# Two channel-major quarters instead of three in some blocks, and Gram products issued one slot after their block

## The chip, the cores and the metric

The kernel runs on one NeuronCore of one Trainium2 chip. A core has a matrix engine (TensorE, PE in the profile, with its weight loads listed apart as PEld), a vector engine (VectorE, DVE), an activation engine (ScalarE, ACT), a general engine (GpSimd, POOL) and a queue engine that only issues transfers (SyncE, SP). Each engine works through its own instructions in order and waits on semaphores for the others. Matrix products land in PSUM, which has eight banks of 128 x 512 fp32; ACT and DVE read them from there.

The metric is device time in microseconds. Smaller is better.

## What is computed

This is one ConvNeXt-V2 block on an image of 512 x 512 pixels with C = 96 channels and E = 384 hidden channels, all in bf16:

```python
out = depthwise 3x3 convolution of x                 # 9 taps, 96 channels
h = (out - mean) / sqrt(var + 1e-5)                   # over the 96 channels of a pixel
h = gelu(h @ w1)                                      # 96 -> 384
gx = sqrt((h * h).sum(over all pixels) + 1e-6)        # one number per hidden channel
nx = gx / (gx.mean(over channels) + 1e-6)
h = grn_gamma * (h * nx) + grn_beta + h
return x + h @ w2                                     # 384 -> 96
```

The line that shapes everything is `gx`: the sum of squares of every hidden channel over the whole image has to be known before the second product can start. So the kernel has a first pass, which ends in `gx`, and a second pass, which makes the output.

## The kernel before

**Blocks and quarters.** The image is cut into 128 blocks of 4 rows (2048 pixels). A block's hidden activations are four quarters of 512 pixels by 384 channels. A quarter is made in one of two layouts. *Channel-major*: hidden channels on the partitions, pixels along the free axis, three products of 128 x 512 with `w1p` stationary. *Pixel-major*: pixels on the partitions, channels along the free axis, six products (384, 128, 256, 256, 128 and 384 columns) with the normalised pixels stationary.

**Two ways to sum squares.** For a channel-major quarter DVE runs three `bn_stats` over 128 x 512 (`entry`, line 672; tile `bst`), which hold mean and variance of 512 pixels. For a pixel-major quarter PE multiplies the activations by themselves: for each of four groups of 128 pixels and each of three groups of channels it issues one 128 x 128 product with the same tile as stationary and as moving operand, and adds it into `gram` in PSUM bank 7; the diagonal is the sum of squares. `gram_next` (line 768) issues such products. One entry of its list `grams` stands for two groups of pixels, so for six products. A pixel-major quarter leaves two entries, twelve products.

**Which block has which.** `cm_quads` (line 100) gives the number of channel-major quarters of block q. Among blocks below 112 it depends on the last digit of q: digits 0, 3, 7 have four ("whole" blocks, whose activations are also stored to memory); digits 1, 4, 8 have two; digits 2, 5, 6, 9 have three. The list of last digits is called a cycle here: ten blocks, ten slots.

**Slots.** The first pass is a loop over slots (`for s in range(last_slot + 1)`). In the steady part a slot does the convolution of block s and the MLP of block s - 14, and the order of the instructions on PE and ACT is written out by hand in the loop's `else` branch: `conv(0)`, `unit(0, 2)`, `unit(2, 1)`, `conv(1)`, `unit(3, 1)`, `unit(4, 2)`, Gram products, `unit(6, 1)`, `unit(7, 1)`, `conv(2)`, `evac`, Gram products, `unit(8, 2)`, `unit(10, 1)`, the sums for the layer norm (`stage_stats`, 24 small products), `unit(11, 1)`. A `unit(bank, n)` fills n PSUM banks with products of the MLP, and ACT applies gelu to them into tile `g`. Units of two banks always use banks 0 and 1; units of one bank take banks 2 and 3 in turn. Each `conv(n)` is a third of the taps (24 products of 64 x 32) into `Y3`, banks 4 to 6, of which there is one copy only: the next slot's `conv(0)` can start when `evac` has copied the banks that it writes into `y_bf`.

**Who copies.** In most slots ACT copies all of `Y3` (128 x 1536). Where the slot's MLP block has two channel-major quarters (`shared`), ACT copies banks 4 and 5 (128 x 1024) and DVE copies bank 6 (128 x 512, the `CAST` rows).

**DVE's order in a slot.** `squares(0)` (2 bn_stats), two transposes of the input for the convolution three slots ahead (`turn_x`), `squares(1)` (2), the copy of bank 6 where shared, `squares(2)` (2), then `squares_rest(2)` (3, if the block has a third channel-major quarter) and the three that a whole block in the slot before still owes. With three in place of four quarters' worth in the slot of a whole block, every slot of a cycle has nine.

**Gram products in a slot.** Each of the two `gram_next` calls takes one entry off the list (six products). A cycle leaves 3 blocks x 4 + 4 blocks x 2 = 20 entries and takes 20, two in each slot; a block's products come up to two slots after it.

**Accounts.** The results of `bn_stats` are kept in groups of 32 entries; when a group is full, `aggregate` condenses it. With `NENT` = 370 entries there are twelve groups, and a thirteenth for the last two blocks. `second_moments`, near the end of the first pass, works over all groups but the last.

**Second pass.** Whole blocks are read back, five blocks are held, and the rest are computed again from the normalised pixels. Its order doesn't depend on `cm_quads` except through which blocks are whole.

In the profile all engine calls of the first pass have the line of a helper (L35), so groups are told apart by operation, tile and shape.

Of the kernel before, what the change touches and what calls it, by code (L numbers as in the profile page):

```python
# [17 lines left out]
BATCH = 4  # L18
NHELD = 5
WHOLE = (0, 3, 7)  # L20
NTAIL = 14
GRB = 3

# [33 lines left out]
def kernel(  # L57
# [23 lines left out]
    NBLK = H // GR  # L81
# [7 lines left out]

    TAIL0 = NBLK - NTAIL  # L90
    HELD = [NBLK - 2 - 2 * i for i in range(NHELD)][::-1]
    KEPT = [NBLK - 5, NBLK - 3, NBLK - 1]

    def is_held(q):
        return q in HELD

    def is_whole(q):
        return q < TAIL0 and q % 10 in WHOLE

    def cm_quads(q):  # L100
        if is_whole(q) or is_held(q):
            return NQ
        if q > HELD[0]:
            return 1
        return 2 if q >= NBLK - 16 or (q - 1) % 10 in WHOLE else 3

    whole = [q for q in range(NBLK) if is_whole(q)]
    g_dram = dram.tile([len(whole), 128, NQ * NCH * QW], bf16, name="g_dram")
# [78 lines left out]
    with ExitStack() as p1:  # L187
# [426 lines left out]
        def stage_rows(k):  # L614
            b0, n = BATCHES[k]
            rt = rts.pop(k)
            N = n * GR * NG
            nq, nt = min(32, N), (N + 31) // 32
            with nc.allow_non_contiguous_dma("small rows of rstd"):
                if nq == 32:  # L620
                    for t in range(nt):
                        sp.dma_start(
                            out=r_dram[b0:b0 + n].rearrange("b r w -> (b r w)").rearrange(
                                "(t q a p) -> t a q p", q=32, a=4, p=32)[t],
                            in_=rt[:, 32 * t:32 * t + 32])
                else:
                    for a in range(4):
                        sp.dma_start(
                            out=r_dram[b0:b0 + n].rearrange("b r (g m) -> (b r g) m", g=NG)[:, 32 * a:32 * a + 32],
                            in_=rt[32 * a:32 * a + nq, :32])  # L630

        def stage_bcast(k):
            b0, n = BATCHES[k]
            rbc = rbcpool.tile([128, BATCH, W], bf16, name="rbc")
            for j in range(GR):
                sp.dma_start(out=rbc[32 * j:32 * j + 32, :n, :].rearrange("p n w -> p (n w)"),
                             in_=bass.AP(r_dram[b0].tensor, r_dram[b0].offset + j * n * W, [[0, 32], [1, n * W]]))
            rbcs[k] = rbc
# [30 lines left out]
        def flat(b):  # L669
            return gs[b].rearrange("p t j w -> p (t j w)")  # L670
# [91 lines left out]
        def square_owed():  # L762
            while owed:
                owed.pop()()

        grams = []

        def gram_next(n):
            for b, c0 in grams[:n]:
                for c1 in (c0, c0 + E):  # L770
                    for j in range(NCH):
                        v = flat(b)[:, c1 + j * 128:c1 + j * 128 + 128]
                        pe.matmul(gram[:, j, :], lhsT=v, rhs=v, start=False, stop=True, skip_group_check=True)
            del grams[:n]
# [63 lines left out]
        for s in range(last_slot + 1):  # L838
            get = lambda kind: at.get((s, kind), [])
            for k in get("rows"):  # L840
                stage_rows(k)
            for k in get("bcast"):
                stage_bcast(k)
            if s + 4 < NBLK:
                load_x(s + 4)
            for b in get("read"):
                stage_read(b)
            for b in get("write"):
                stage_write(b)
            store_next()  # L850
            for k in get("newton"):
                stage_newton(k, pool)
            for b in get("sqp"):
                stage_sq(b, False)
            for b in get("norm"):
                stage_norm(b)
            for k in get("rstd"):
                stage_rstd(k, pool)
            mlp = get("mlp")

            def spread_out():
                for k in get("spread"):
                    stage_spread(k)
                for b in get("norma"):
                    stage_norm(b, dve if b < 2 else pool)

            spare = not mlp and s % 2 == 1
            taps, evac = conv_taps(s, spare) if s < NBLK else ([], None)
            if mlp and mlp[0] >= TAIL0:
                assert not taps  # L870
                square_owed()
                mlp_tail(mlp[0], get)
            elif not mlp:
                if s + 3 < NBLK:
                    turn_x(s + 3)
                for f in taps:
                    f()
                if not spare:
                    spread_out()
                if evac:  # L880
                    evac()
                for b in get("sqa"):
                    stage_sq(b, True)
                for b in get("stats"):
                    stage_stats(b)
                for k in get("moments"):
                    stage_moments(k)
                if spare:
                    spread_out()
                for k in get("chain"):  # L890
                    stage_moments(k)
                    stage_chain(k)
                for k in get("turn"):
                    stage_turn(k)
                gram_next(2)
                square_owed()
            else:
                b = mlp[0]
                unit, squares, squares_rest = mlp_units(b)
                conv = lambda n, fence=True: taps[n](fence) if taps else None  # L900

                conv(0)
                unit(0, 2)
                unit(2, 1)
                squares(0)
                conv(1, False)
                spread_out()
                if s + 3 < NBLK:
                    turn_x(s + 3)
                unit(3, 1)  # L910
                unit(4, 2)
                squares(1)
                gram_next(1 if taps else 2)
                shared = evac is not None and cm_quads(b) == 2
                unit(6, 1)
                if not shared:
                    squares(2)
                unit(7, 1)
                for k in get("turn"):
                    stage_turn(k)  # L920
                conv(2)
                if evac:
                    evac(shared)
                if shared:
                    squares(2)
                gram_next(1 if taps else 2)
                unit(8, 2)
                unit(10, 1)
                for b2 in get("stats"):
                    stage_stats(b2)  # L930
                unit(11, 1)
                for k in get("moments"):
                    stage_moments(k)
                squares_rest(2)
                square_owed()
                if is_whole(b):
                    owed.append(lambda f=squares_rest: f(3))
                grams.extend((b, c) for c in range(cm_quads(b) * QC, NQ * QC, 2 * E))
                if is_whole(b):
                    stores.extend((b, h) for h in range(3))  # L940
            if s == 0:
                setup_ynt()
            if s == 3:
                setup_mlp()
            if s == 4:
                setup_rest()
            if s == 6:
                for i in range(NI):
                    sp.dma_start(out=w1s[i:128:4], in_=w1p[i:C:NI])
            for b in get("combine"):  # L950
                combine(b)
            if s == last_slot - 3:
                pc.close()
                late.xr = p2.enter_context(tc.tile_pool(name="xr", side="right", bufs=5))
                late.xb = p2.enter_context(tc.tile_pool(name="xb", side="right", bufs=3))
                late.gr = p2.enter_context(tc.tile_pool(name="gr", side="right", bufs=GRB))
                late.gl = p2.enter_context(tc.tile_pool(name="gld", side="right", bufs=2))
                late.o = p2.enter_context(tc.tile_pool(name="o", side="right", bufs=4))
            if s == last_slot - 2:
                for n in range(PRE):  # L960
                    load_xr(n, sp)
                second_moments(0, NACC - 1)
            if s == last_slot - 1:
                for n in range(3):
                    stage_xb(ORDER[n], pool, B2bc_f)
            if s == last_slot:
                for n in range(PRE):
                    load_rest(n, sp, sp)
# [102 lines left out]
```

## Time and profile before

| what | value |
|---|---|
| median of 3 runs | 1471.92 us (1469.99 to 1472.07) |
| the profiled execution's own time | 1470.01 us |
| its span in the profile | 1468.2 us |
| mean granted TensorE clock | 0.995 |
| PE busy over the span | 1392.9 us (95%) |
| ACT busy over the span | 1404.5 us (96%) |
| POOL busy over the span | 1300.0 us (89%) |
| DVE busy over the span | 1187.7 us (81%) |
| DVE `bn_stats`, 128 x 512 | 1110, 673.5 us busy |
| PE Gram products, 128 x 128 (`PS<-g`) | 1464, 123.4 us busy |
| DVE copies of bank 6 (`CAST y_bf<-PS`) | 35, 23.5 us busy |

The shares of busy time are averages over two passes with different limits. The first pass ends with the first products of the second at about 964 us; its steady part, with a convolution and an MLP in every slot, lies between about 200 and 867 us. There a slot starts with the first of three rows `MATMUL PS<-xT,Wq ... x24` in the time-ordered view of PE and ends where the next slot's first such row starts.

### The profile page before, as it was taken

What the parts mean: (1) busy time and instruction counts of PE and PEld (TensorE: products, weight loads), DVE (VectorE), ACT (ScalarE), POOL (GpSimd) and SP (SyncE); (2) the same over time, 40 slices, a digit from 0 to 9 for tenths busy, and PEclk for the clock granted to TensorE, in tenths of its full rate; (3) what the DMA queues carried; (4) which work ended last, traced back from release to release, by engine and by line L of the source; (5) the groups of instructions that cost most, each with busy time, mean ns of one, the idle gap of its engine ahead of it and who ended that gap; (6) DMA issues with size and microseconds to landing.
All of it is one profiled execution on the core that took longest, in us unless ns stands there. A gap on an engine that the chain in (4) does not pass through costs nothing.

```text
span 1468.2 us, 54503 instructions
## 1 busy us (share of the span) xinstructions
PE 1392.9 (95%) x23125; PEld 811.3 (55%) x23125; DVE 1187.7 (81%) x2174; ACT 1404.5 (96%) x1595; POOL 1300.0 (89%) x923
## 2 busy tenths in 40 slices
PE   8889999999999999999999998779999999999998
PEld 3434444444444444444444455557777777777776
DVE  8859989999999999999999997965555555555555
ACT  7889999999999999999999999989999999999997
POOL 3479889999999999999899997449999999999998
PEclk9999999999999999999999999999999999999999
DMA  6578878788888888888889876649999999999998
GB/s 181 178 218 241 264 236 279 244 262 262 266 263 275 259 250 269 266 272 255 269 246 284 256 226 200 197 161 375 358 329 387 396 390 399 400 385 408 385 395 311
DMA packets 167914, 422.03 MB, mean 287 GB/s; under 512 B 34327, under 2 KB 84183, under 8 KB 163191
## 3 DMA queue, kind: packets, MB, share of 16 engines
q1 hardware_dynamic: 151428, 314.98, 66.1%
q0 software_dynamic: 14880, 103.43, 18.6%
q8 instruction: 181, 2.97, 0.8%
q14 instruction: 63, 0.51, 0.1%
q10 hardware_dynamic: 1362, 0.15, 0.1%
HBM read 262.16 MB, written 156.22 MB: 285 GB/s over the span
## 4 chain that ended last, share of the span: by engine, by line
DVE 36%; PE 28%; POOL 14%; ACT 13%; issue 4%; DMA 2%; SPq 2%; ACTq 0%; POOLq 0%; DVEq 0%
PE PS L35 28%; DVE bst L35 25%; POOL xb L328 11%; ACT g L35 9%; DVE xT L35 7%; ACT y_bf L35 3%; SPq L35 2%; POOL xr L283 1%; DVE y_bf L35 1%; DMA yn_dram<-yn 1%; POOL yn L35 1%; DVE o_sb L35 1%; DMA ynT<-yn_dram 1%; ACT xT L35 1%; DVE parts L35 1%
## 5 line engine op out<-in xcount | busy, mean ns | idle before, releaser
L35 ACT ACTIVATE g<-PS 128x512 bf16<-128x512 f32 (+2 forms) x1062 | 730.0, 845 | 12.9 <-PE PS L35 9.9
L35 DVE BATCH_NORM_STATS2 bst<-g 128x6 f32<-128x512 bf16 x1110 | 673.5, 673 | 26.2 <-ACT g L35 26.0
L35 ACT ACTIVATE gr<-PS 128x1536 bf16<-128x1536 f32 x360 | 498.5, 1457 | 20.8 <-PE PS L35 9.7
L35 DVE TENSOR_TENSOR o_sb<-PS,xb 128x384 bf16<-128x384 f32 x512 | 277.6, 556 | 222.0 <-PE PS L35 170.0
L35 POOL TENSOR_TENSOR yn<-y_bf,rbc 128x1536 bf16<-128x1536 bf16 x126 | 391.0, 3106 | 45.4 <-ACT rbc L35 21.7
L328 POOL TENSOR_TENSOR xb<-xr,B2c 128x1536 f32<-128x1536 bf16 x118 | 368.2, 3133 | 1.5
L35 PE MATMUL PS<-xT,Wq 64*32 64x511 bf16 (+1 forms) x9198 | 345.4, 387 | 21.7 <-ACT y_bf L35 6.4
L35 PE MATMUL PS<-ynT,w1p 128*128 128x512 bf16 x1161 | 332.5, 383 | 22.9 <-ACT g L35 5.4
L35 POOL TENSOR_TENSOR ysq<-y_bf 128x1536 bf16<-128x1536 bf16 x114 | 313.0, 2746 | 30.7 <-ACT y_bf L35 16.7
L35 PE MATMUL PS<-ynT,w1s 128*128 128x512 bf16 x1020 | 275.6, 379 | 0.0
L35 PEld LDWEIGHTS <-gr 128*128 128x128 bf16 x4296 | 212.5, 98 | 61.3 <-issue 3.2
L35 PE MATMUL PS<-W2s,gr 128*128 128x96 bf16 x4224 | 223.8, 206 | 1.9 <-DVE o_sb L35 1.8
L35 PEld LDWEIGHTS <-Wq 64*32 64x32 bf16 x9216 | 111.7, 90 | 191.1 <-issue 148.8
L35 ACT ACTIVATE y_bf<-PS 128x1536 bf16<-128x1536 f32 (+2 forms) x135 | 182.1, 1354 | 16.8 <-PE PS L35 12.6
L35 DVE STREAM_TRANSPOSE xT<-xin 128x576 f32<-128x576 f32 (+1 forms) x256 | 181.6, 749 | 14.7 <-DMA xin<-in_x_dram 14.7
L35 PEld LDWEIGHTS <-w1p 128*128 128x128 bf16 x1161 | 89.9, 98 | 178.9 <-issue 116.0
L35 PEld LDWEIGHTS <-g 128*128 128x128 bf16 (+1 forms) x1707 | 105.7, 98 | 88.3 <-issue 56.1
L35 PE MATMUL PS<-w1p,ynT 128*128 128x256 bf16 (+2 forms) x822 | 125.7, 273 | 7.7 <-ACT xT L35 3.2
L35 PE MATMUL PS<-g 128*128 128x128 bf16 x1464 | 123.4, 221 | 3.5 <-DVE PS L35 3.5
L35 PEld LDWEIGHTS <-w1s 128*128 128x128 bf16 x1020 | 82.0, 98 | 40.5
L35 PEld LDWEIGHTS <-gl 128*128 128x128 bf16 x1680 | 83.1, 98 | 29.7 <-issue 8.5
L35 PE MATMUL PS<-W2s,gl 128*128 128x96 bf16 x1680 | 90.3, 206 | 5.0 <-DVE o_sb L35 4.3
(109 smaller groups left out, 714.1 us busy)
## 6 DMA issues: line engine op xcount, KB each, us to landing
xin<-in_x_dram SPq DMA_DIRECT2D x126, 432.0 KB
g_dram<-g SPq DMA_DIRECT2D x105, 512.0 KB
gl<-g_dram POOLq DMA_DIRECT2D x35, 1536.0 KB, 10.9
yn_dram<-yn SPq DMA_DIRECT2D x512, 96.0 KB
ynT<-yn_dram SPq DMA_DIRECT2D x128, 384.0 KB
out_dram<-o_sb SPq DMA_DIRECT2D x127, 384.0 KB
xr<-in_x_dram POOLq DMA_DIRECT2D x123, 384.0 KB, 6.8
ynT<-yn_dram SPq DMA_DIRECT2D x255, 128.0 KB
```

The lines of the kernel that those rows point to most:

```text
L35: r = f(*a, **k)
L283: pq.dma_start(out=xr[:], in_=x[0, r0:r0 + GR].rearrange("r w c -> (r w) c").rearrange("(p g) c -> p g c", g=PXP))
L328: pq.tensor_tensor(out=xb[:], in0=grp[q]["xr"][:], in1=bias[:, None, :].to_broadcast([128, PXP, C]), op=ALU.add)
```

## The change

`cm_quads` gets a list of its own for blocks with two channel-major quarters: last digits 1, 4, 5, 8, 9. So digits 5 and 9 go from three to two, and only 2 and 6 have three. Below block 112 this concerns 22 blocks. In their slots, `shared` is now true too. The two calls of `gram_next` no longer take one entry each: the first takes half of what is on the list (rounded up), the second the rest.

```diff
+TWOS = (1, 4, 5, 8, 9)
...
-        return 2 if q >= NBLK - 16 or (q - 1) % 10 in WHOLE else 3
+        return 2 if q >= NBLK - 16 or q % 10 in TWOS else 3
...
                 squares(1)
-                gram_next(1 if taps else 2)
+                gram_next((len(grams) + 1) // 2)
                 shared = evac is not None and cm_quads(b) == 2
                 unit(6, 1)
...
                 if shared:
                     squares(2)
-                gram_next(1 if taps else 2)
+                gram_next(len(grams))
                 unit(8, 2)
```

A cycle now leaves 5 blocks x 4 + 2 blocks x 2 = 24 entries. Since the list is empty at the end of every slot's second call, a slot issues what the block before it left. By the last digit of the slot's MLP block:

| digit | 0 | 1 | 2 | 3 | 4 | 5 | 6 | 7 | 8 | 9 |
|---|---|---|---|---|---|---|---|---|---|---|
| channel-major quarters before | 4 | 2 | 3 | 4 | 2 | 3 | 3 | 4 | 2 | 3 |
| channel-major quarters after | 4 | 2 | 3 | 4 | 2 | 2 | 3 | 4 | 2 | 2 |
| Gram entries in the slot before | 2 | 2 | 2 | 2 | 2 | 2 | 2 | 2 | 2 | 2 |
| Gram entries in the slot after | 4 | 0 | 4 | 2 | 0 | 4 | 4 | 2 | 0 | 4 |

`NENT` falls from 370 to 348, and with it the groups from twelve and one to eleven and one.

## The prediction

> **What bounds the kernel now.** I first took the busy times of the engines by stretches of 100 us. From 300 to 800 us every stretch looks like this one (columns: PE, PEld, DVE, ACT, POOL busy, granted clock, DMA):
>
> ```profile
> 500.00:600.00 100.00, 97.15 (x1769) 47.52 (x1765) 99.69 (x176) 99.05 (x144) 93.65 (x77) 1.00 0.86 262
> ```
>
> Four engines are nearly full, so the average names no bound. The chain that ended last, for 500 to 560 us, names DVE:
>
> ```profile
> by line: DVE bst L35 68.1%; DVE xT L35 20.2%; issue 4.7%; DVE y_bf L35 2.9%; DVE mom L35 1.4%; PE PS L35 1.3%; DVE rt L35 0.6%; DVE PS L35 0.6%; DVE tot L35 0.5%
> ```
>
> A chain can run along any engine that is full, so I then read PE slot by slot. First the slot of a two-quarter block:
>
> ```profile
> 500.83 0.89 PE L35 MATMUL PS<-xT,Wq 64*32 64x512 bf16 x24
> ...
> 504.08 0.50 PE L35 MATMUL PS<-g 128*128 128x128 bf16 x6
> 504.41 0.60 PE L35 MATMUL PS<-w1p,ynT 128*128 128x384 bf16 x4
> 504.94 0.87 PE L35 MATMUL PS<-xT,Wq 64*32 64x512 bf16 x24
> 505.74 0.51 PE L35 MATMUL PS<-g 128*128 128x128 bf16 x6
> 506.09 0.82 PE L35 MATMUL PS<-w1p,ynT 128*128 128x128 bf16 x6
> ```
>
> The next slot starts at 507.65, so this one lasted 6.82 us, without a stated wait: PE is the limit. Each six Gram products move what follows by 0.33 to 0.35 us. Slots that copy all of `Y3` on ACT last 7.03 us; from 514.92:
>
> ```profile
> 521.42 0.38 PE L35 MATMUL PS<-ynT,w1p 128*128 128x512 bf16 x1
> 521.95 0.88 PE L35 MATMUL PS<-xT,Wq 64*32 64x512 bf16 x24 [0.16 <-ACT y_bf L35]
> ```
>
> Here PE is done early and waits for ACT's copy (520.35, 1.55 us long, so to 521.90). This is a loop, not a full engine: taps, first unit, six gelu calls, copy, next taps.
>
> DVE comes in at one place, its copy of bank 6, which it reaches late:
>
> ```profile
> 509.07 0.65 DVE L35 CAST y_bf<-PS 128x512 bf16<-128x512 f32 x1
> ...
> 509.40 1.27 PE L35 MATMUL PS<-xT,Wq 64*32 64x512 bf16 x24
> ```
>
> The second row of taps needs that bank; it takes 1.27 instead of 0.88 us, and the slot from 507.65 7.27 us. The nine cycles from 213.34 to 846.15 (starts of the slots of blocks 20 and 110) average 70.3 us. With undisturbed slots (7.03 four times; three times each 6.82 and the 6.98 of the slot behind it when DVE is on time, as from 578.23 to 585.21) a cycle would be 69.5: DVE costs 0.8 us per cycle.
>
> Last, a slot that already has what the change makes three times a cycle, a two-quarter block without any Gram product:
>
> ```profile
> 199.70 0.89 PE L35 MATMUL PS<-xT,Wq 64*32 64x512 bf16 x24 [0.67 <-ACT y_bf L35]
> ...
> 203.00 0.87 PE L35 MATMUL PS<-w1p,ynT 128*128 128x384 bf16 x4
> 203.81 0.88 PE L35 MATMUL PS<-xT,Wq 64*32 64x512 bf16 x24
> 204.62 0.83 PE L35 MATMUL PS<-w1p,ynT 128*128 128x128 bf16 x6
> 205.28 0.45 PE L35 MATMUL PS<-rowsel,y_bf 128*128 128x4 bf16 x12
> ```
>
> and the next slot begins at 206.31. It lasted 6.61, not 6.82 - 0.67 = 6.15: ACT's short copy (205.07, 1.18 us long, to 206.25) holds the next taps. PE's lead is lost there.
>
> **The change part by part.**
>
> *DVE.* Each of 22 blocks loses three bn_stats and gains one copy of bank 6. Nine bn_stats in a row take 5.40 us with one of 0.67 at the end, so 0.59 each from start to start, and the copy as much: -1.19 us per block, -26 us in all. The stretch of nine cycles has DVE busy 630.5 of 632.8 us, 70.1 per cycle; it becomes 67.7. DVE is then no longer late, and the 0.8 us per cycle of waits goes; what is late next is PE and the copy loop, so no more than that is gained. In undisturbed slots the copy starts about 0.1 us into the next slot and a start up to 1.0 us there delays nothing, which is the cover for the two further copies; if it is gone, each costs 0.4 us as above.
>
> *ACT.* 22 copies shrink from 128x1536 to 128x1024. ACT's wait for PE grows instead; the gain is that `Y3` is free sooner, which counts only where PE isn't the limit.
>
> *PE, quarters.* Three products of 512 columns become six with as many columns; the two layouts cost the same (0.65 us per quarter, from start to start): nothing. Its six weight loads in place of three lie beside products.
>
> *PE, Gram products.* Twelve more per changed block, 264 in all; and the four entries of a block now fall into one slot. Within a six the starts are (0.50 - 0.22)/5 = 0.056 us apart, and six move the rest by 0.33; twelve more in a slot cost 0.67. No row shows twelve in a run. The lower end is 0.66, two sixes at 0.33, and nothing at all if the 6.82 held a wait that they could fill, for which no row speaks. The upper end is 0.88, from the chain's first piece of the second pass, where 627 products of mixed shapes, most of them with a new stationary tile each, take 45.95 us, 0.073 each. I take 0.67, since shape and stage are the same. The Trainium skill, "TensorE: Matmul & The Clock Gate", section on the back-to-back issue gap, says that in a stream of loads and products the spacing at 128 columns is about 81 ns, with 56 ns only for isolated ones; this trace has 56 in such a stream of six. By 81 ns the heavy slots below would be 0.3 us longer, and the estimate some 17 us higher.
>
> *Slots of the changed cycle.* Heavy slots (digits 0, 2, 5, 6, 9; four entries): PE's own work, 6.80 (6.79 to 6.82 in slots where PE is the limit), + 0.67 = 7.47. Is anything else later? The first six extra products put `unit(6, 1)` at 504.41 - 500.83 + 0.33 = 3.91 us into the slot and its result at 4.4, where ACT asks for it at 4.5; the taps end in time for the copy at 5.4; a full copy frees `Y3` at 7.03, before 7.47. So PE alone sets it, and the 0.2 us that PE waited in full-copy slots is used up. Light slots (digits 1, 4, 8; no entries): 6.61, measured above. Digits 3 and 7: as before, 7.03. A cycle: 5 x 7.47 + 3 x 6.61 + 2 x 7.03 = 71.24 against 70.3, with the gain from DVE already in it.
>
> *New waits.* The products read `g` of the block before; its last gelu ends 1.7 us into the slot, the first portion comes at 3.2. None. `g` buffers come free earlier. SP's and POOL's orders are untouched; POOL is busy 600.8 of 632.8 us, 66.8 per cycle, and lags in light slots only to catch up in heavy ones.
>
> *Sum.* Nine cycles: 9 x 71.24 - 632.81 = +8.3. Blocks 6 to 15, from 107.58 to 178.07, 70.5 before: 71.24, +0.8. Block 19, heavy for 7.03: +0.4. Blocks 110 to 113, 27.6 before: three heavy, one light, 29.0, +1.4. Block 5, in a slot of 8.5 us with other waits: between 0 and 0.67, +0.3. Blocks 16 to 18: none. At the end of the first pass one group of accounts fewer: three `parts` operations in the chain (942.07 to 950.01, 7.9 us) go from 12 to 11 groups, -0.7; the dropped `aggregate`, 0.8, lies in DVE's slack. Together +10.5. The second pass is untouched. The profiled execution took 1470.0 us (span 1468.2), so 1480.5 against its own time; the median of the three runs is 1.9 higher, so 1482.4.
>
> **The rivals.**
>
> *Light slots make up for heavy ones (faster).* If PE could carry its lead over, only its total would count: ten slots of 6.80 + four entries of 0.33 = 69.3 per cycle, 1.0 less than now, about -10 us with the rest: 1462. For it: PE may run ahead by the units' free banks. Against: the 6.61 slot, after which PE stood still for the copy. It decides if light slots come out near 6.15. Chance 0.10, and 0.05 for a half-way case, about no change.
>
> *DVE sets the pace throughout (faster).* Then the full 26 us would come: 1446. For it: 99.7% and the chain. Against: PE in slots without a late copy, 6.82 with no wait. Chance 0.04. The Trainium skill, "Perfetto Trace Analysis", on identifying the most-contended engine, goes this way: the engine with the highest occupancy is to be relieved first. The trace agrees on DVE's occupancy, not that it alone sets the time.
>
> *Late copies stay, or twelve products cost more (slower still).* Five copies a cycle at 0.4 us each would be +22 us, 1504; products at 0.073 us would be +0.21 x 5 x 11 = +12, 1494. Chance 0.08.
>
> **How the numbers follow.** Forecast 0.73, with 1477 to 1489 as its own range (heavy slots of 7.40 to 7.55); the rivals as above. I name 1482. The range, 1474 to 1493, leaves out the faster cases (0.14) and the end of the last. What a measurement can't tell from no change is 0.2%, 2.9 us: slower 0.81, same 0.05, faster 0.14.
>
> **What would show it.** Right: slots of 7.4 to 7.5 us with two runs of twelve Gram products, 6.6 where there are none, the second row of taps always near 0.88, DVE with visible waits for `g`, no wait of PE for ACT's copy in the heavy slots. Wrong: light slots near 6.15, or heavy ones below 7.2 (then something in the 6.80 was a wait that the products cover), or copies of bank 6 that still come over 1 us into the next slot.

## The result and the profile after

The changed kernel takes 1480.01 us (median of 6, 1478.78 to 1482.49) against 1470.78 for the kernel before beside it (1469.66 to 1472.07): ratio 1.0061, 95% interval 1.0048 to 1.0073. On another occasion the ratio was 1.0057, interval 1.0037 to 1.0077. So it is slower by about 0.6%, 8 to 9 us. The profiled execution took 1482.49 us, its span is 1480.4.

In time-ordered rows of PE, the slot of a two-quarter block with digit 1 (from 509.57) and the slots of digits 5 and 6 (from 537.14 and 544.65) look like this; columns are start, duration, operation and tiles, and the last row of the first is cut by the end of the view:

```profile
509.57 0.87 PE L36 MATMUL PS<-xT,Wq 64*32 64x512 bf16 x24
...
516.07 0.61 PE L36 MATMUL PS<-xT,Wq 64*32 64x512 bf16 x9
```

```profile
537.14 0.87 PE L36 MATMUL PS<-xT,Wq 64*32 64x512 bf16 x24
538.13 0.82 PE L36 MATMUL PS<-ynT,w1p 128*128 128x512 bf16 x3
538.88 0.86 PE L36 MATMUL PS<-xT,Wq 64*32 64x512 bf16 x24
539.68 0.87 PE L36 MATMUL PS<-ynT,w1p 128*128 128x512 bf16 x3
540.39 0.83 PE L36 MATMUL PS<-g 128*128 128x128 bf16 x12
541.06 0.60 PE L36 MATMUL PS<-w1p,ynT 128*128 128x384 bf16 x4
541.59 0.88 PE L36 MATMUL PS<-xT,Wq 64*32 64x512 bf16 x24
542.40 0.84 PE L36 MATMUL PS<-g 128*128 128x128 bf16 x12
543.08 0.82 PE L36 MATMUL PS<-w1p,ynT 128*128 128x128 bf16 x6
...
544.65 0.88 PE L36 MATMUL PS<-xT,Wq 64*32 64x512 bf16 x24
```

The light slot lasts 6.50 us, the heavy one 7.51. Twelve Gram products move what follows by 0.67 us (540.39 to 541.06) and 0.68 (542.40 to 543.08). Nothing in the heavy slot waits; the second row of taps is at its 0.86, so no copy is late. The copy behind the light slot stands at 0.05 us into the next slot, in DVE's rows:

```profile
516.12 0.65 DVE L36 CAST y_bf<-PS 128x512 bf16<-128x512 f32 x1
```

DVE has slack now, and the chain has left it. First the row of stretches for 500 to 600 us, then the chain for 500 to 560:

```profile
500.00:600.00 100.00, 97.57 (x1779) 49.32 (x1778) 95.53 (x169) 96.74 (x142) 93.16 (x76) 1.00 0.85 268
```

```profile
by line: PE PS L36 52.4%; ACT g L36 27.8%; ACT y_bf L36 10.8%; DMA ynT<-yn_dram 6.4%; issue 3.2%; ACTq L36 0.1%
```

DVE fell from 99.69 to 95.53, ACT from 99.05 to 96.74, and PE is where the chain goes. In the view of waits over the nine cycles (218.10 to 857.10) DVE waits for activations (columns: us in total, times, longest); the same view of the kernel before has no such row over its nine cycles:

```profile
DVE bst L36 <- ACT g L36: 22.2, 33, 1.1
```

Slot by slot, from the starts of such rows in the two profiles (the median of the ten or eleven slots of each digit, blocks 6 to 112):

| slots by last digit of the MLP block | 0 | 1 | 2 | 3 | 4 | 5 | 6 | 7 | 8 | 9 | sum |
|---|---|---|---|---|---|---|---|---|---|---|---|
| before, median us | 7.03 | 6.82 | 6.99 | 7.03 | 6.83 | 7.11 | 7.03 | 7.03 | 6.83 | 7.24 | 69.94 |
| after, median us | 7.44 | 6.50 | 7.49 | 6.98 | 6.61 | 7.50 | 7.44 | 6.93 | 6.61 | 7.50 | 71.00 |
| after minus before | 0.41 | -0.32 | 0.50 | -0.05 | -0.22 | 0.39 | 0.41 | -0.10 | -0.22 | 0.26 | 1.06 |

The nine cycles took 632.8 us before and 639.0 after. The medians before add up to less than 70.3 because late copies are no median's business: they come in some cycles and not in others.

### The profile page after: what moved, and what is told of

Read it like the earlier page. It is cut to its first block, busy times and chain, and to the rows that moved or that the text cites. A ratio compares the mean times of both kernels' runs of the same rounds, so it can differ in the third digit from the quotient of the medians.

```text
span 1480.4 us, 55117 instructions
## 1 busy us (share of the span) xinstructions
PE 1407.1 (95%) x23455; PEld 828.0 (56%) x23455; DVE 1167.0 (79%) x2126; ACT 1397.3 (94%) x1595; POOL 1299.8 (88%) x923
## 4 chain that ended last, share of the span: by engine, by line
PE 40%; ACT 23%; POOL 17%; DMA 9%; issue 4%; DVE 4%; SPq 2%; ACTq 0%; POOLq 0%; DVEq 0%
PE PS L36 40%; ACT g L36 16%; POOL xb L329 12%; DMA yn_dram<-yn 5%; ACT y_bf L36 5%; SPq L36 2%; POOL yn L36 2%; DVE bst L36 1%; POOL xr L284 1%; ACT xT L36 1%; DMA ynT<-yn_dram 1%; DMA g_dram<-g 1%; POOL ysq L36 1%; DMA out_dram<-o_sb 1%; DMA xin<-in_x_dram 1%
## 5 line engine op out<-in xcount | busy, mean ns | idle before, releaser
L36 DVE BATCH_NORM_STATS2 bst<-g 128x6 f32<-128x512 bf16 x1044 | 639.6, 674 | 58.1 <-ACT g L36 57.4
L36 PE MATMUL PS<-xT,Wq 64*32 64x511 bf16 (+1 forms) x9198 | 340.2, 388 | 14.2 <-ACT y_bf L36 3.3
L36 PE MATMUL PS<-ynT,w1p 128*128 128x512 bf16 x1095 | 312.5, 385 | 24.6 <-ACT g L36 5.0
L36 PEld LDWEIGHTS <-Wq 64*32 64x32 bf16 x9216 | 107.9, 90 | 177.0 <-issue 137.4
L36 ACT ACTIVATE y_bf<-PS 128x1024 bf16<-128x1024 f32 (+2 forms) x135 | 170.1, 1266 | 19.9 <-PE PS L36 14.5
L36 PEld LDWEIGHTS <-w1p 128*128 128x128 bf16 x1095 | 84.6, 98 | 181.0 <-issue 130.2
L36 PE MATMUL PS<-w1p,ynT 128*128 128x384 bf16 (+1 forms) x954 | 148.3, 272 | 11.9 <-ACT xT L36 3.2
L36 PEld LDWEIGHTS <-g 128*128 128x128 bf16 (+1 forms) x1971 | 116.6, 98 | 62.4 <-issue 36.9
L36 PEld LDWEIGHTS <-ynT 128*128 128x128 bf16 x954 | 74.3, 97 | 62.0 <-issue 39.0
```

Of the source, the lines that this page charges most:

```text
L36: r = f(*a, **k)
```

## The experiments

A cycle is counted as in the prediction: nine of them, from the start of the slot of block 20 to that of block 110. Two theories stood against each other at the outset. The slot theory: each slot is the larger of PE's own work and the wait for the copy of `Y3`, nothing is carried over, so gathering the products in some slots is what costs. Its rivals: the quarters themselves cost it, or part of the loss isn't in the slots at all, since 7.5 us of the 12.2 by which the span grew lay in the first 100 us, where both kernels do the same.

**The second half of the change alone.**

```diff
-                gram_next(1 if taps else 2)
+                gram_next((len(grams) + 1) // 2)
...
-                gram_next(1 if taps else 2)
+                gram_next(len(grams))
```

> Only the second half of the change: the quarters are those of the kernel before, the Gram products of a block all come in the next slot. 20 entries per cycle: four in the slots of digits 2, 5, 9, none in those of 1, 4, 8, two in the others. Theory of the slots (each slot is the larger of PE's own work, 6.13 us and 0.333 per entry, and the wait for the copy, 6.95 with a full and 6.55 with a short copy): 3 x 7.47 + 3 x 6.55 + 4 x 6.97 = 69.9 per cycle while DVE is on time. DVE needs about 70.1 per cycle, so the late copies of bank 6 stay: 70.2 to 70.8 per cycle, total within 0.3% of the kernel before. Rival (light slots make up for heavy ones): 68.3 on PE alone, so DVE's 70.1 decides and the total is that of the kernel before or lower. Rival (gathering the products costs what the change costs): about +9 us.

Measured: 633.0 us for nine cycles, 70.3 each, ratio 1.0009 (0.9990 to 1.0028). The slots are those of the theory: 7.48 to 7.50 with four entries, 6.61 without, 6.98 to 7.03 with two. But one expectation failed: the late copies of bank 6 did not stay, although DVE is as busy as before (630.7 of the 633.0 us). In the kernel before, the second rows of taps together run over 0.9 us by 0.80 us per cycle; here it is 0.07, because the copies come on average 0.5 to 0.9 us into the next slot, not 1.0 to 1.4. In a slot behind one of digit 1, for instance, which starts at 510.93:

```profile
511.64 0.65 DVE L35 CAST y_bf<-PS 128x512 bf16<-128x512 f32 x1
```

```profile
512.67 0.88 PE L35 MATMUL PS<-xT,Wq 64*32 64x512 bf16 x24
```

So gathering 20 entries is not free, it comes out even: against the version with DVE relieved alone (below: 69.6 per cycle, the same products two entries to a slot, no late copies) the gathered slots cost 0.7 us per cycle, and the end of the late copies gives as much back.

**The quarters of the change, with the products spread.**

```diff
+TAKE = (3, 1, 3, 3, 1, 2, 3, 3, 2, 3)
...
-                gram_next((len(grams) + 1) // 2)
+                take = TAKE[b % 10] if taps and b >= 10 else len(grams)
+                gram_next((take + 1) // 2)
...
-                gram_next(len(grams))
+                gram_next(take // 2)
```

> The quarters of the change, but the products spread: from block 10 on a slot takes, by the last digit of its block from 0 to 9, 3, 1, 3, 3, 1, 2, 3, 3, 2, 3 entries off the list instead of all (24 per cycle as in the change). Theory of the slots: full-copy slots with three entries 6.13 + 1.0 = 7.13; short-copy slots with one 6.5, with two 6.80, with three 7.13; a cycle is 5 x 7.13 + 2 x 6.55 + 2 x 6.80 + 7.13 = 69.5, 1.5 less than the change's 71.0 and 0.8 less than the 70.3 of the kernel before; 16 us faster than the change and 7 to 9 us faster than the kernel before (ratio 0.994 to 0.996). Rival (the quarters themselves cost it: 264 more products on a full PE): the spread gains nothing, ratio 1.004 to 1.008 as with the change.

Measured: 626.7 us for nine cycles, 69.6 each; 1466.41 us, ratio 0.9965 (0.9945 to 0.9986), faster than the kernel before, by 6 us where 7 to 9 were expected. The nine cycles hold 11341 products of PE in this kernel and in the changed one; the only difference is in which slot the Gram products stand. Two slots of it, digits 5 and 6:

```profile
460.12 0.88 PE L37 MATMUL PS<-xT,Wq 64*32 64x512 bf16 x24
...
463.36 0.50 PE L37 MATMUL PS<-g 128*128 128x128 bf16 x6
...
465.02 0.51 PE L37 MATMUL PS<-g 128*128 128x128 bf16 x6
...
466.94 0.89 PE L37 MATMUL PS<-xT,Wq 64*32 64x512 bf16 x24
...
470.17 0.83 PE L37 MATMUL PS<-g 128*128 128x128 bf16 x12
...
472.17 0.51 PE L37 MATMUL PS<-g 128*128 128x128 bf16 x6
...
474.08 0.42 PE L37 MATMUL PS<-xT,Wq 64*32 64x512 bf16 x8
```

6.82 us with two entries, 7.14 with three. The rival (the quarters cost it) has fallen. The 0.1 us per cycle over the expected 69.5 comes from the slot of digit 6, which in four of the cycles was about 7.65, behind a copy that came 1.4 to 1.6 us into the slot, as in these rows of DVE and PE, where the slot starts at 744.59:

```profile
745.96 0.68 DVE L37 CAST y_bf<-PS 128x512 bf16<-128x512 f32 x1
```

```profile
746.35 1.22 PE L37 MATMUL PS<-xT,Wq 64*32 64x512 bf16 x24
```

**The spread version with digit 6 in place of 5.**

```diff
-TWOS = (1, 4, 5, 8, 9)
+TWOS = (1, 4, 6, 8, 9)
-TAKE = (3, 1, 3, 3, 1, 2, 3, 3, 2, 3)
+TAKE = (3, 2, 3, 3, 1, 3, 2, 3, 2, 2)
```

> The spread version with two edits: the blocks with two channel-major quarters have last digits 1, 4, 6, 8, 9, and a slot takes 3, 2, 3, 3, 1, 3, 2, 3, 2, 2 entries. In the first spread version the slot of digit 6 was 0.5 us late in some cycles, after a late copy of bank 6; here two short-copy slots with nine bn_stats and no relief between them are further apart. Theory of the slots: 5 x 7.12 + 4 x 6.80 + 6.51 = 69.3 per cycle, 1.0 less than the kernel before; 9 to 11 us faster than that (ratio 0.992 to 0.995), 0 to 4 us faster than the first spread version. Rival (no further gain, since something other than PE limits): as the first, 0.9965.

Measured: 627.9 us for nine cycles, 69.8 each; ratio 0.9958 (0.9941 to 0.9975), 1464.44 us. It beats both kernels, but by about 6 us over the kernel before, not the 9 to 11 expected, and not the first spread version beyond the intervals: no further gain is shown, as the rival had it. Most of its slots have the expected times (7.10, 6.78, 7.14, 7.10, 6.51, 7.15, 6.79, 7.12, 6.79, 6.79). Three are 8.0 to 8.5, behind late copies, and the first of them, from 389.06 to 397.55, has a new cause, in the rows of DVE and PE:

```profile
388.93 1.44 DVE L37 STREAM_TRANSPOSE xT<-xin 128x576 f32<-128x576 f32 x2 [2.38 <-DMA xin<-in_x_dram]
...
391.45 0.67 DVE L37 CAST y_bf<-PS 128x512 bf16<-128x512 f32 x1
```

```profile
392.18 0.87 PE L37 MATMUL PS<-xT,Wq 64*32 64x512 bf16 x23 [0.99 <-DVE y_bf L37]
```

DVE waited 2.38 us for the input's transfer, the copy behind it was late, and PE waited for the copy. Over the nine cycles DVE waits 5.9 us for such transfers here; in the first spread version the view of waits has no such row. Whether the edit brought this on or one execution's transfers did, one profile can't say.

**DVE relieved alone.** In the kernel before:

```diff
         def entry(b, j, m):
+            w = 16 if m == 2 and b < 112 and b % 10 in (5, 9) else QW
...
-            dve.bn_stats(out=bsts[k][:, j, e, :], in_=gs[b][:, m, j, :])
+            dve.bn_stats(out=bsts[k][:, j, e, :], in_=gs[b][:, m, j, :w])
```

> The kernel before with DVE relieved alone: the three bn_stats of the third quarter in blocks with last digit 5 or 9 run over 16 instead of 512 columns (the sum of squares then lacks most of these pixels); no quarter and no product is changed. DVE's need per cycle falls from 70.1 by about 3 us. Theory of the slots: only the late copies of bank 6 go, 0.8 us per cycle: 69.5 per cycle, 8 to 10 us faster than the kernel before (ratio 0.993 to 0.995). Rival (DVE sets the pace throughout): 67 per cycle, 30 us faster. Rival (DVE is nowhere the limit): no change.

Measured: 626.6 us for nine cycles, 69.6 each; ratio 0.9935 (0.9920 to 0.9949), 10 us faster. The nine cycles give 6.2 of these, 0.69 us per cycle, where 0.8 was expected and the rival needed 3; where the rest lies, one profile doesn't tell. DVE's busy time over the nine cycles fell from 630.5 to 607.6 us, 2.5 per cycle. The chain for 500 to 560 us shows what takes over:

```profile
by line: PE PS L35 36.7%; ACT g L35 30.1%; ACT y_bf L35 14.5%; DMA yn_dram<-yn 13.8%; issue 4.0%; POOL nt L35 1.1%; SPq L35 0.5%; ACTq L35 0.2%
```

So with the other limits where they are, the gain that the change can draw from DVE is this 0.7 us per cycle, whatever its need falls by.

**The changed kernel without the products.**

```diff
+                if taps and b >= 10:
+                    del grams[:]
                 gram_next((len(grams) + 1) // 2)
```

> The changed kernel with the Gram products of the slots from block 10 to 113 left out (the sum of squares then lacks these pixels). Theory of the slots: PE is no longer the limit anywhere, what is left is the wait for the copy: 6.93 to 6.98 in full-copy slots, 6.50 to 6.61 in short-copy ones, 67.5 per cycle unless DVE, which needs 67.7, becomes the limit again (up to 68.5); 26 to 36 us faster than the change. Rival (the products are hidden, the loss comes from elsewhere): within 10 us of the change.

Measured: 621.4 us for nine cycles, 69.0 each, 17.6 less than the changed kernel; 1458.36 us in all, 24 less than that kernel's first profiled execution, a little under the range. The floors came out at 7.03 for a full and 6.61 for a short copy, which makes 68.2 per cycle, and late copies and input transfers come on top; DVE is busy 611.7 of these 621.4 us. It shows what all 24 entries cost the changed kernel on balance, 2.0 us per cycle (on balance, because late copies came back here, in slots of digits 0 and 6 of up to 7.8 us); and that below 69 us the next limits are near: the copy loop, DVE, and then POOL (598.4).

In PE's rows one sees the loop bare; a slot from 427.32 to 433.92 whose start waited, and one that waits at its end:

```profile
427.32 0.87 PE L36 MATMUL PS<-xT,Wq 64*32 64x512 bf16 x24 [0.48 <-ACT y_bf L36]
...
433.92 0.89 PE L36 MATMUL PS<-xT,Wq 64*32 64x512 bf16 x24
...
440.96 0.42 PE L36 MATMUL PS<-xT,Wq 64*32 64x512 bf16 x8 [0.48 <-ACT y_bf L36]
```

**The start-up.** The two kernels, unchanged, profiled again:

> The kernel before, profiled a second time, to see how far its first 100 us differ from one execution to the next. In the profile shown, the slot of block 17 starts at 92.6 us, and the clock is granted in full up to there. Theory A (start-up varies by itself): the start of that slot moves by some us between executions, and the part from there to the second pass repeats within 1 us: 632.8 us for the nine cycles, 7.03, 6.82 and 7.0 to 7.5 us per slot. Theory B (the start-up belongs to the kernel): it starts at 92 to 94 us again, with no half-clock stretch.

> The changed kernel, profiled a second time. In its first profile, 7.5 us of the 12.2 us by which its span was longer lay before the slot that does the convolution of block 17 (100.1 instead of 92.6 us), where both kernels issue the same work; the granted clock was 0.50 from 36 to 40 us. Theory A (start-up varies by itself): this time the slot starts anywhere between 92 and 101 us, and the nine cycles take 639 us again. Theory B (the start-up belongs to the kernel): about 100 us with the half-clock stretch again.

> The changed kernel once more, timed in more rounds on another occasion, for the size of the loss and for its start-up. From the slots (+5 us between the slot of block 17 and the second pass in the first two profiles) the ratio should be about 1.003 to 1.005 if the later start of that slot (98.7 and 100.1 us, against 92.6 and 93.8 before) was chance, and about 1.006 to 1.008 if the start-up of this kernel is longer every time; the slot then starts at 98 to 100 us again, else anywhere from 92 to 100.

> The kernel before, a third profile, for its start-up. So far the slot of block 17 starts at 92.6 and 93.8 us here (and at 92.8 in the version with DVE relieved alone), without a half-clock stretch before it, but at 93.1, 98.7 and 100.1 in the changed kernel and at 96.3 to 98.9 in four others, with one where it is late. If start-up varies by itself, a half-clock stretch and a start over 95 us should turn up here too, in one of two tries or so; if it belongs to the changed kernels, 92 to 94 us again.

> The same, a fourth profile: over 95 us with a half-clock stretch in the first 100 us if start-up varies by itself, 92 to 94 if not.

> The changed kernel, a fourth profile beside them: the nine cycles 639 us again; the slot of block 17 anywhere from 92 to 101 us.

| kernel, profile | start of the slot of the convolution of block 17 | from there to that of block 127 | nine cycles | from there to the end |
|---|---|---|---|---|
| before, 1 | 92.6 | 774.2 | 632.8 | 601.4 |
| before, 2 | 93.8 | 773.0 | 632.8 | 601.4 |
| before, 3 | 97.7 | 772.8 | 632.8 | 593.6 |
| before, 4 | 99.2 | 772.8 | 632.8 | 601.2 |
| after, 1 | 100.1 | 778.5 | 639.0 | 601.9 |
| after, 2 | 98.7 | 781.0 | 639.2 | 600.4 |
| after, 3 | 93.1 | 780.6 | 639.2 | 602.6 |
| after, 4 | 99.9 | 779.9 | 639.2 | 600.8 |

The start-up varies by itself: by 6.6 us among the four profiles of the kernel before, and by 7.0 among those of the changed one. The nine cycles repeat within 0.2 us. From the slot of block 17 to that of 127 the means are 773.2 and 780.0: the change costs 6.8 us there, 0.46%. Of the two timed differences, the interval of the second (5.4 to 11.3 us) holds these 6.8, that of the first (7.1 to 10.7) just misses them. The mean spans of the four profiles differ by 10.9 us. Of what goes beyond 6.8, 2.1 us lie before the slot of block 17, where the changed kernel fell on the late side in three of four profiles and the kernel before in two of four; that this is chance is likely from the table, not proven by it. The other 2.0 lie behind the slot of block 127, and nearly all of them come from the third profile of the kernel before (the next section and the last show what it is).

## Why the prediction was right, and where it wasn't

**The bound.** PE's own work and the copy loop were named, not DVE's 99.7%. The run with DVE relieved alone confirms it: 2.5 us per cycle taken from DVE's busy time brought 0.7.

**Heavy slots: 7.47.** Measured 7.44 to 7.50. The twelve products cost 0.67 and 0.68 for a run of twelve, as two sixes; the upper end of 0.88 didn't come. 0.67/12 is 56 ns, in a run in which every product has a new stationary tile. The 81 ns of the Trainium skill, "TensorE: Matmul & The Clock Gate", section on the back-to-back issue gap, didn't come either. Two readings of the prediction were wrong without harm. Its trace does have a run of twelve at full clock, as long as those measured after, which could have sized the cost directly:

```profile
48.78 0.83 PE L35 MATMUL PS<-g 128*128 128x128 bf16 x12
```

And no slot of that trace lasts 6.79: the undisturbed slots that PE limits take 6.82 to 6.84. With 6.82 the sum is 7.49, as in the slots of digits 2, 5 and 9; those of 0 and 6 took 7.44.

**Light slots: 6.61.** Measured 6.61 for digits 4 and 8, 6.50 for digit 1. No lead was carried over, so the rival of 1462 fell; but the spread version shows that it was right in its sum: by its working 69.3 per cycle is what PE needs, and 69.6 is reached if the products, not the lead, are moved.

**Digits 3 and 7: 7.03.** Measured 6.98 and 6.93. The step that failed is "as before": these slots come behind a heavy slot now, and their loop is a little shorter. The link that is shorter is ACT's copy. It starts where it did, about 5.4 us into the slot, but takes 1.51 us (medians) where it took 1.55 (digit 3) and 1.61 (digit 7). First a slot of digit 7 before (from 542.89), then the same slot after (from 552.09), in ACT's rows:

```profile
548.26 1.61 ACT L35 ACTIVATE y_bf<-PS 128x1536 bf16<-128x1536 f32 x1
```

```profile
557.46 1.51 ACT L36 ACTIVATE y_bf<-PS 128x1536 bf16<-128x1536 f32 x1
```

In the slot of digit 1, also behind a heavy one, it takes 1.08, against 1.19 in that of digit 4. The run that only gathers agrees: its digits 0, 3 and 6, behind heavy slots, have a copy of 1.51 and last 6.98 or 6.99, its digit 7, behind a slot with two entries, 1.61 and 7.03. In all these shorter slots ACT has waited 0.25 to 0.38 us before; why the copy is then shorter, no run shows. With digit 1's 0.11 this makes the cycle 71.0 instead of 71.24 and the nine cycles +6.3 instead of +8.3.

**DVE's late copies go.** They did: the second row of taps is 0.86 to 0.90 in every slot of the nine cycles, and the 0.8 us per cycle, 0.69 by experiment, is in the balance. It is why the loss is 0.7 per cycle and not 1.4. The reason given, that DVE has less to do, is enough, as the run with DVE relieved alone shows, but it isn't the only one: gathering alone took the late copies from 0.80 to 0.07 us per cycle. The two work together in the change, and no run tells their shares.

**Blocks before 20: +1.5.** This term was wrong. From the slot of the convolution of block 17 to that of 34 the four profiles average 119.7 before and 119.4 after, so -0.3, with up to 2.4 us between profiles of one kernel. One place is the same in all: the slots of the convolutions of blocks 28 and 29 took 7.90 and 5.94 or 5.95 before (6.52 in the first profile, where a stretch at half clock falls into the second slot) and 7.64 to 7.67 and 4.94 to 4.96 after. In the second of them, which has no MLP, PE waits for DVE, and block 15 has left DVE three bn_stats fewer: in the version with DVE relieved alone, where block 15 has them shortened, this slot takes 4.95 too. The term had costed the heavy and light slots only, not this one.

**One group of accounts fewer: -0.7.** Not there. The three `parts` operations took 1.71, 3.08 and 3.08 us before; after, in the chain:

```profile
952.82 2.06 DVE parts L36
954.90 3.07 DVE parts L36
958.00 3.07 DVE parts L36
```

Their time doesn't follow the number of groups: 72 columns before and 66 after take the same. It follows POOL. In the first profile of the kernel before three operations of POOL lie beside them, and each `parts` ends 0.1 us behind one of these (POOL's end at 943.66, 946.76 and 949.86):

```profile
940.53 9.33 POOL L35 TENSOR_TENSOR xb<-xr,B2bc_f 128x1536 f32<-128x1536 bf16 x3 [16.77 <-DVE bst L35]
```

```profile
941.99 1.79 DVE L35 TENSOR_TENSOR parts<-mom 128x72 f32<-128x72 f32 x1
943.81 6.17 DVE L35 TENSOR_TENSOR parts<-parts,mom 128x72 f32<-128x72 f32 x2
```

In the third profile of the same kernel DVE was done before POOL began (947.04), and each took about a quarter of a microsecond:

```profile
944.46 0.25 DVE L35 TENSOR_TENSOR parts<-mom 128x72 f32<-128x72 f32 x1
944.75 0.54 DVE L35 TENSOR_TENSOR parts<-parts,mom 128x72 f32<-128x72 f32 x2
```

All thirteen profiles of this case agree: each of these operations that falls beside POOL's ends 0.1 us behind one, and the seven that don't take 0.23 to 0.26. No run tries it by an edit, and by which path POOL holds DVE up isn't shown.

**The sum.** +10.5 was forecast, from slots and the accounts; the slots give +6.8 (+6.3 in the nine cycles, -0.3 before them, +0.8 in the three slots behind them) and the timing 8 to 9. The mechanism was right: heavy slots at PE's own work, light ones at the copy, nothing carried over. What was mis-sized are four terms: the cycle by 0.2 us, the blocks before 20, those behind the nine cycles and the group of accounts. That the time came within 2.4 us of the 1482 named is partly luck: what the timing has beyond 6.8 belongs to no term of the sum.

## What to carry to other kernels

Where the engines meet once per slot at a single buffer, price a change slot by slot: the larger of each engine's work and the wait at the buffer, and don't add up engines over a cycle, since a lead made in a light slot is lost at the next meeting. Work without a deadline, like these Gram products, belongs in the slots that have room for it; the same 24 entries cost 1.4 us per cycle more when each block's are issued in the next slot than when they are spread. And an engine at 99.7% may be worth no more than its late arrivals: relieving it by 2.5 us per cycle brought 0.7.

## What the runs showed of the hardware

The start of a program and the gap between its passes are not the same from one execution to the next. In the view by stretches, the granted clock of the kernel before was 1.00 between 32 and 36 us in one profile and half for most of it in another (first the third profile, then the fourth):

```profile
32.00:36.00 4.00, 3.06 (x39) 1.32 (x40) 4.00 (x9) 3.00 (x5) 2.02 (x1) 1.00 0.89 263
```

```profile
32.00:36.00 4.00, 3.68 (x36) 1.42 (x37) 3.22 (x11) 1.51 (x2) 0.00 (x0) 0.57 0.80 216
```

In the fourth profile the first unit of that slot had waited for a transfer, and its three products took 1.44 instead of 0.81 us:

```profile
32.32 1.44 PE L35 MATMUL PS<-ynT,w1p 128*128 128x512 bf16 x3 [1.44 <-DMA ynT<-yn_dram]
```

That slot (convolution of block 5) takes 9.2 us at full clock in four of the eight profiles of the two kernels and 11.1 to 13.9 in the four that have a half-clock stretch there. The start-up as a whole goes with such stretches: of the thirteen profiles of this case, the four without one between 10 us and the slot of block 17 start that slot at 92.6 to 93.8 us, the nine with one at 96.3 to 100.1. Which of the two brings the other is not shown: in the fourth profile the slot of block 5 began 1.4 us later than in the first, before the stretch there. The lengths of the stretches are 3.41, 6.83, 10.24 and 13.65 us. These are multiples of the window of 3413 ns, running freely, that the Trainium skill, "TensorE: Matmul & The Clock Gate", section "What's actually happening", gives.

Between the passes seven of the eight profiles have a stretch of 6.8 or 10.2 us; the third profile of the kernel before has none, and from the slot of block 127 to the end it took 593.6 us instead of about 601. But the clock is the smaller part of that. In this profile the three `parts` operations ran before POOL's and took 0.8 us together, where they took 7.9 to 8.4 in the seven others. From the last step of `gx` to the end it took 503.5 us, against 503.8 to 506.1.

The spans of the four profiles of the kernel before run from 1464.1 to 1473.2 us. So a few executions of one kernel may differ by 9 us for reasons that have nothing to do with an edit, and a change of under 1% is better read from a stretch that repeats, as the nine cycles do.
